# A delta-rule attention kernel: the score product is split into keys with keys, early, and keys with queries and state, late

## The chip, the cores and the metric

The kernel runs on one core of a Trainium2 chip. The metric is the device time of one execution in microseconds (us), from the first to the last instruction. Data are float32, except for the two weight matrices of the second block, which arrive as float64 and are converted inside the kernel.

## The reference, cut to what matters

Two blocks follow each other. The first is a linear attention with a delta rule: 4 batches, 8 heads, 768 time steps, head dimension 48. The second is a two-layer network with a quick GELU on the 3072 x 384 result.

```python
k_n = k / (norm(k) + 1e-6)
for t in range(S):                                   # S = 768
    y[t]  = q[t] @ state                             # state: D x D per batch and head, D = 48
    v_old = k_n[t] @ state
    state = state + beta[t] * outer(k_n[t], v[t] - v_old)
x = y, heads side by side                            # (4*768) x 384
h = x @ w_in                                         # 384 x 2048
out = (h * sigmoid(1.702 * h)) @ w_out               # 2048 x 384
```

The kernel works on chunks of 128 time steps. A **unit** is one chunk of one batch with its 8 heads; there are 6 chunks x 4 batches = 24 units, and units 0 to 3 are the first chunk, where the state is still zero. Inside a chunk the recurrence becomes a triangular system. It needs the products of keys with keys (matrix N, from which 32 x 32 diagonal blocks are inverted), of keys with queries (masked to the part above the diagonal), of keys with the old state (subtracted from the values), and of queries with the old state.

## The kernel before

The start normalizes the keys of units 0 to 3, prepares these four units, and inverts their diagonal blocks (a substitution, one VectorE operation after another). Then a loop of slots runs. Slot n holds the later part of unit n-1, the middle of unit n and the start of unit n+1, the preparation of unit n+4, and pieces of the two-layer network ("filler") in between; each slot has six groups.

```python
W0, W1, WB = 3, 1, (1, 3, 5, 7, 8)       # weight parts to convert: at the start, after the inversion, per slot
NW, NA0, NY, NB0 = 80, 3, 48, 6          # matmuls that only keep TensorE busy; NB0 per group of the first slots

for i in range(B):                        # first loads: keys on SyncE's queue, queries on ScalarE's
    for t, src, dma in ((KN, k, nc.sync.dma_start), (QP, q, nc.scalar.dma_start)):
        nc.vector.memset(t[i][:, :, D:DP], 0.0)
        load(i, ((t, src),), dma)

def prepare(n):
    c, b = units[n]
    kn, qp = KN[n % len(KN)], QP[n % len(QP)]
    kqT = wk.tile([128, NP, 2, 128], F32, tag="kqT", bufs=6)
    for i, src in enumerate((kn, qp)):                       # keys, then queries
        psT = ...                                            # one PSUM bank
        for j in range(NP):                                  # NP = 4 pairs of heads
            pe.transpose(psT[:, j, :], flat[:, j * 128 : (j + 1) * 128], ident)
        act.activation(kqT[:, :, i, :], psT, ACT.Copy)
        yield 0.6
    G = wk.tile([128, H, 2, 128], F32, tag="G", bufs=6)
    for g in range(0, NP, 2):
        ps = [two banks, "psG"]
        for i in range(2):
            for hh in range(2):                              # even and odd heads: partitions 0.. and 64..
                pr = slice(hh * 64, hh * 64 + D)
                pe.matmul(ps[hh][:, i], lhsT=kqT[pr, g + i, 0, :], rhs=kqT[pr, g + i, :, :])   # 256 columns
        act.activation(G[:, 2 * g : 2 * g + 4 : 2], ps[0], ACT.Copy)
        if n < HB or B <= n < 2 * B + HB:
            act.activation(G[:, 2 * g + 1 : 2 * g + 4 : 2], ps[1], ACT.Copy)
        else:
            vec.tensor_copy(G[:, 2 * g + 1 : 2 * g + 4 : 2], ps[1])
        yield 1.0
    nc.sync.dma_start(out=Nd..., in_=G[:, :, 0, :])          # N to DRAM
    nc.sync.dma_start(out=NT[...], in_=Nd...)                # its diagonal blocks back, one per partition
    nc.gpsimd.affine_select(out=G[:, :, 1, :], ...)          # mask of the queries' scores

# class Step (one unit)
def keys(self):                                              # not for the first chunk
    for h in range(H):
        pe.matmul(psK[h % 2][:, j, :], lhsT=self.kqT[self.rows(h), j, 0, :],
                  rhs=ST[self.rows(h), self.b, j * D : (j + 1) * D])                           # 48 columns
    for hh in range(2):
        vec.tensor_tensor(Vh, Vh, psK[hh], op=ALU.subtract)

def slot(n, share):
    for group in range(GR):                                  # GR = 6
        if group == 0:   next(P, None); next(P, None)        # P = prepare(n + 4): transposes
        elif group == 1: together([(B_, 1)], [(A, 2)]); next(P, None)
        elif group == 2: D_ = steps[n + 1] = Step(n + 1, ...); D_.keys(); run(P)
        elif group == 3: together([(A, 3), (D_, 0)], [(B_, 1)])
        elif group == 4: A.queries(); A.outputs()
        else:            together([(B_, 2)], [(D_, 0)]); A.state()
        ...
        more = left // (GR - group)                          # left starts as WB[n + 1]
        run(weights(more)); left -= more                     # convert weight parts
        ... filler ...
        if not queue and n <= HB:
            warm(NB0)
    ...
    load(m, ((KN, k), (QP, q)), ...)                         # m = n + 6

# the start
for b in range(0, B, HB):
    normalize_first(b)
ahead(1, sync)                                               # first three weight parts, one transfer
run(weights(1, None))                                        # convert part 0
first = [prepare(b) for b in range(B)]
for b in range(B + 1):
    if b < B:
        next(first[b]); next(first[b]); warm(NA0)
    if b > 0:
        run(first[b - 1])
run(weights(W0 - 1, None))                                   # convert parts 1 and 2
for b in range(B):
    load_values(b, sync)
...
ahead(2, sync)                                               # fetch further weight parts
run(invert(0))
normalize_first(B, len(KN) - B)
run(weights(W1))
for n in range(-1, len(units) + 1):
    slot(n, ...)
```

A `together` call solves blocks (psU), copies the result (US), multiplies it with the rows below (psR) and subtracts that from the values V on VectorE. Up to slot 1 the instructions of VectorE, ScalarE and TensorE are held in program order. The conversion of a weight part is a handful of VectorE operations (in most parts one on ScalarE); the raw part waits in a staging place inside the buffer of w_out, and a place is free again once the part after it has been converted.

Of the kernel before, what the change touches and what calls it, by code (L numbers as in the profile page):

```python
# [18 lines left out]
def kernel(  # L19
# [37 lines left out]

    W0, W1, WB = 3, 1, (1, 3, 5, 7, 8)
    NA = W0

    NW, NA0, NY, NB0 = 80, 3, 48, 6
    XR = DP - D
# [57 lines left out]
    for i in range(B):  # L120
        for t, src, dma in ((KN, k, nc.sync.dma_start), (QP, q, nc.scalar.dma_start)):
            nc.vector.memset(t[i][:, :, D:DP], 0.0)
            load(i, ((t, src),), dma)

# [87 lines left out]
    def stage(part):  # L212
# [11 lines left out]
        return at, at + 2 * DM  # L224

    def free(part):
        s = stage(part)
        return s is None or all(s[1] <= a or b <= s[0] for a, b in taken.values())

    def fetch(part, dma):  # L230

        if part < parts_in:
            j, f0 = part % KC, part // KC * N_IN
            parts = list(range(part, part + (KC if part < 3 * KC else 1)))
            shape, src = (len(parts), N_IN), moe_w_in[:, f0 : f0 + N_IN]
            dst = w_in[:, j : j + len(parts), f0 : f0 + N_IN]
        else:
            parts = [part]
            shape, src = (1, DM), moe_w_out
            dst = target(part)  # L240
# [75 lines left out]
    def normalize_first(b0, nb=HB):  # L316
# [5 lines left out]
        z = wk.tile([128, 4, nb, H], F32, tag="ksq", name="z", bufs=1)  # L322
        sq = wk.tile([128, nb, H, D], F32, tag="G", name="sq", bufs=6)
        x, y, t, s = (z[:, i] for i in range(4))
        for b in range(nb):
            K = KN[(b0 + b) % len(KN)][:, :, 0:D]
            tt(sq[:, b], K, K, op=mult)
            red(s[:, b], sq[:, b], axis=AX.X, op=add)
        ts(x, s, 1e-30, None, op0=ALU.max)
# [8 lines left out]
        for b in range(nb):  # L338
            K = KN[(b0 + b) % len(KN)][:, :, 0:D]
            tt(K, K, s[:, b].broadcast_to([128, H, D]), op=mult)  # L340

    def prepare(n):
        c, b = units[n]
        kn, qp = KN[n % len(KN)], QP[n % len(QP)]

        kqT = wk.tile([128, NP, 2, 128], F32, tag="kqT", name="kqT", bufs=6)
        for i, src in enumerate((kn, qp)):
            if c == 0:
                psT = ps_seq.tile([128, NP, 128], F32, tag="seq", name="psT")
            else:  # L350
                psT = ps_big.tile([128, NP, 128], F32, tag="big", name="psT")
            flat = src.rearrange("p h d -> p (h d)")
            for j in range(NP):
                pe.transpose(psT[:, j, :], flat[:, j * 128 : (j + 1) * 128], ident)  # L354
            act.activation(kqT[:, :, i, :], psT, ACT.Copy)
            yield 0.6


        G = wk.tile([128, H, 2, 128], F32, tag="G", name="G", bufs=6)
        for g in range(0, NP, 2):  # L360
            if c == 0 and g > 0:
                ps = [ps_moe.tile([128, 2, 2, 128], F32, tag="moe", name="psG") for _ in range(2)]
            else:
                ps = [ps_big.tile([128, 2, 2, 128], F32, tag="big", name="psG") for _ in range(2)]
            for i in range(2):
                for hh in range(2):
                    pr = slice(hh * 64, hh * 64 + D)
                    pe.matmul(  # L368
                        ps[hh][:, i], lhsT=kqT[pr, g + i, 0, :], rhs=kqT[pr, g + i, :, :],
                        start=True, stop=True,  # L370
                    )
            act.activation(G[:, 2 * g : 2 * g + 4 : 2], ps[0], ACT.Copy)  # L372
            if n < HB or B <= n < 2 * B + HB:
                act.activation(G[:, 2 * g + 1 : 2 * g + 4 : 2], ps[1], ACT.Copy)
            else:
                vec.tensor_copy(G[:, 2 * g + 1 : 2 * g + 4 : 2], ps[1])  # L376
            yield 1.0

        Nd = dram.tile([H * NS], F32, tag="Nd", name="Nd", bufs=4)
        nc.sync.dma_start(  # L380
            out=Nd.rearrange("(h r) -> h r", r=NS)[:, 0 : C * C].rearrange(
                "h (p k) -> p h k", k=C
            ),
            in_=G[:, :, 0, :],
        )
        nc.sync.dma_start(
            out=NT[b * NB * H : (b + 1) * NB * H],
            in_=Nd.rearrange("(d r) -> d r", r=NS // NB)[:, 0 : BS * C].rearrange(
                "d (i k) -> d i k", k=C
            )[:, :, 0:BS],  # L390
        )
        nc.gpsimd.affine_select(  # L392
            out=G[:, :, 1, :], in_=G[:, :, 1, :], compare_op=ALU.is_gt, fill=0.0, base=0,
            pattern=[[0, H], [1, 128]], channel_multiplier=-1,
        )
        ready[n] = kn, kqT, G

# [90 lines left out]
    class Step:  # L488
# [6 lines left out]
        def __init__(self, n, xT):  # L495
            self.c, self.b = units[n]
            self.xT = xT
            self.kn, self.kqT, self.G = ready.pop(n)
            self.V, self.XB = loaded.pop(n), inverse.pop(n)
            self.US = US[n % len(US)]  # L500
            self.U = self.US[:, 0 : H * D].rearrange("p (h d) -> p h d", h=H)

        def rows(self, h):
            return slice(h % 2 * 64, h % 2 * 64 + D)

        def keys(self):
            if self.c == 0:
                return
            psK = [bank("psK", (128, NP, D)) for _ in range(2)]
            for h in range(H):  # L510
                j = h // 2
                pe.matmul(  # L512
                    psK[h % 2][:, j, :], lhsT=self.kqT[self.rows(h), j, 0, :],
                    rhs=ST[self.rows(h), self.b, j * D : (j + 1) * D], start=True, stop=True,
                )
            for hh in range(2):
                Vh = self.V[:, hh::2, :]
                vec.tensor_tensor(Vh, Vh, psK[hh], op=ALU.subtract)

        def below(self, blk, h, psR):  # L520
            r = slice(blk * BS, (blk + 1) * BS)
            for k in range(blk + 1, NB):
                u = slice(k * BS, (k + 1) * BS)
                pe.matmul(  # L524
                    psR[u, h, :], lhsT=self.G[r, h, 0, u], rhs=self.U[r, h, :],
                    start=True, stop=True,
                )
# [5 lines left out]
        def solve(self, blk, h, psU):  # L533
            r = slice(blk * BS, (blk + 1) * BS)
            pe.matmul(  # L535
                psU[r, h, :], lhsT=self.XB[r, h, :], rhs=self.V[r, h, :],
                start=True, stop=True,
# [18 lines left out]
        def queries(self):  # L556
            self.psY = [bank("psY", (128, 2, 128)) for _ in range(2)]
            if self.c > 0:
# [3 lines left out]
                    lambda h: ST[self.rows(h), self.b, h // 2 * D : h // 2 * D + DP],  # L562
                    lambda h: self.kqT[self.rows(h), h // 2, 1, :],
                    True,
# [15 lines left out]
        def outputs(self):  # L580
            self.turned(
                (0, 4, 1, 5, 2, 6, 3, 7),
                lambda h: self.US[:, h * D : h * D + DP], lambda h: self.G[:, h, 1, :],
                self.c == 0,
# [93 lines left out]
    steps, xTs, inverting, gT0 = {}, {}, iter(()), []  # L678

    def together(solves, belows):  # L680

# [14 lines left out]
    def slot(n, share):  # L696
# [12 lines left out]
        for group in range(GR):  # L709
            if group == 0:  # L710
                next(P, None)
                next(P, None)
            elif group == 1:
                together([(B_, 1)], [(A, 2)])
                next(P, None)
            elif group == 2:
                if n + 1 < len(units):
                    h = (n + 1) // HB
                    if h not in xTs:
                        xTs[h] = wk.tile([128, KC, NTH], F32, tag="xT", name="xT", bufs=3)  # L720
                    D_ = steps[n + 1] = Step(n + 1, xTs[h])
                    D_.keys()
                run(P)
            elif group == 3:
                together([(A, 3), (D_, 0)], [(B_, 1)])
            elif group == 4:
                if A:
# [12 lines left out]
            ahead_of(inverting, 5 if n % HB == 1 else 4)  # L740
            more = left // (GR - group)
            run(weights(more))
# [8 lines left out]
        if n % HB == 0:  # L751
            run(inverting)
        if n > 0:
            m = n - 1 + len(KN)
            if m < len(units):
                load(m, ((KN, k), (QP, q)), sync if n < B else nc.sync.dma_start)
            if n - 1 + B < len(units):
# [14 lines left out]
    for b in range(0, B, HB):  # L772
        normalize_first(b)
    ahead(1, sync)
    run(weights(1, None))
    first = [prepare(b) for b in range(B)]
    for b in range(B + 1):
        if b < B:
            next(first[b])
            next(first[b])  # L780
            warm(NA0)
        if b > 0:
            run(first[b - 1])
    run(weights(W0 - 1, None))
    for b in range(B):
        load_values(b, sync)
    nc.gpsimd.memset(ST, 0.0)
    for U in US:
# [3 lines left out]
    for i in range(B, len(KN)):  # L792
        load(i, ((KN, k), (QP, q)), sync)
    ahead(2, sync)
# [38 lines left out]
```

## Time and profile before

| what | value |
|---|---|
| time, median of three | 843.53 us (841.94 to 843.6) |
| profiled execution | 838.2 us, mean granted TensorE clock 0.959 |
| busy: TensorE matmul | 780.8 us (93%) |
| busy: VectorE / ScalarE / GpSimd | 489.2 (58%) / 200.3 (24%) / 109.8 us (13%) |
| first operation of the inversion | 41.24 us after the start |
| its last operation (scaling by beta) starts | 66.47 us |
| first solve of a block (psU) | 77.25 us |
| transposes of unit 6, which open slot 2 | 110.02 us |

Shares over the whole span hide that the program has stages. The page's strip of 40 slices shows TensorE idle or at reduced clock in the first seventh and busy throughout after that, so the table gives the moments at which the early stages end. "PE" is TensorE's matmuls, "PEld" its weight loads, "DVE" VectorE, "ACT" ScalarE, "POOL" GpSimd, "SPq" SyncE's DMA queue. In the trace each float32 matmul of the code stands as two instructions, and each float32 transpose as one.

### The profile page before, as it was taken

How to read it: one execution, taken by the hardware profiler on the slowest of the kernel's cores; microseconds unless marked ns; L12 is line 12 of the kernel's file. 1: busy time of each engine (PE TensorE's matmuls, PEld its weight loads, DVE VectorE, ACT ScalarE, POOL GpSimd, SP SyncE). 2: the span in 40 equal slices, each digit the busy share in tenths (PEclk: the TensorE clock that was granted, in tenths of full speed). 3: DMA queues.
4: the chain of work that ended last, by engine and by line, in shares of the span. 5: the costliest groups of instructions: out<-in, count | busy, mean ns of one | idle time of the engine just before them, and what ended most of it. 6: DMA issues, size and time to landing. Idle time of an engine off the chain costs nothing.

```text
span 838.2 us, 18516 instructions
## 1 busy us (share of the span) xinstructions
PE 780.8 (93%) x8036; PEld 569.2 (68%) x8036; DVE 489.2 (58%) x1049; ACT 200.3 (24%) x383; POOL 109.8 (13%) x120
## 2 busy tenths in 40 slices
PE   8307789999899999999999999999999999999998
PEld 7206578766666876866867867867767768677684
DVE  5698779978977484584584592692781851110000
ACT  3201454242221321221321322312312202111020
POOL 2102231151020211121021112102100000000000
PEclk9657879999899999999999999999999999999999
DMA  9698373553214204214214213223122020000000
GB/s 147 156 159 161 79 188 90 111 146 75 51 36 89 63 20 101 53 44 85 52 36 84 61 41 76 44 51 75 27 67 65 3 52 9 10 16 1 24 1 19
DMA packets 160976, 55.95 MB, mean 67 GB/s; under 512 B 128672, under 2 KB 157568, under 8 KB 160896
## 3 DMA queue, kind: packets, MB, share of 16 engines
q1 hardware_dynamic: 154048, 46.02, 27.5%
q0 software_dynamic: 1856, 7.87, 3.0%
q10 hardware_dynamic: 4992, 0.89, 1.0%
q8 instruction: 63, 1.03, 0.5%
q14 instruction: 17, 0.14, 0.1%
HBM read 33.13 MB, written 20.45 MB: 64 GB/s over the span
## 4 chain that ended last, share of the span: by engine, by line
PE 74%; DVE 12%; DMA 7%; issue 3%; POOL 2%; SPq 1%; ACT 0%; ACTq 0%; DVEq 0%; POOLq 0%
PE po L631 28%; PE ph L616 27%; PE psG L368 4%; PE psU L535 4%; PE psY L551 4%; DMA w_out<-in_moe_w_out_dram 2%; PE psK L512 2%; DVE P L104 2%; PE psR L524 2%; PE psT L354 1%; DMA w_out<-in_moe_w_in_dram 1%; DMA QP<-in_q_dram 1%; DVE YB L104 1%; DVE w_in L104 1%; PE psS L573 1%
## 5 line engine op out<-in xcount | busy, mean ns | idle before, releaser
L616 PE MATMUL ph<-xT,w_in 128*128 128x256 f32 (+1 forms) x1248 | 273.9, 373 | 0.8 <-DVE o L638 0.4
L631 PE MATMUL po<-w_out,gT 128*128 128x384 f32 x768 | 268.3, 495 | 1.8 <-DVE w_out L194 1.8
L616 PEld LDWEIGHTS ph<-xT,w_in 128*128 128x128 f32 x1248 | 221.7, 194 | 39.8 <-issue 9.3
L631 PEld LDWEIGHTS po<-w_out,gT 128*128 128x128 f32 x768 | 139.8, 190 | 94.0 <-issue 6.8
L621 ACT ACTIVATE gT<-ph 128x512 f32<-128x512 f32 (+1 forms) x104 | 58.5, 564 | 186.3 <-PE ph L616 186.3
L531 DVE TENSOR_TENSOR V<-V,psR 32x384 f32<-32x384 f32 x87 | 48.3, 556 | 91.5 <-PE psR L524 89.6
L542 ACT COPY US<-psU 32x384 f32<-32x384 f32 x88 | 41.3, 469 | 166.4 <-PE psR L524 148.1
L535 PEld LDWEIGHTS psU<-V,XB 32*32 32x32 f32 x1408 | 50.5, 106 | 30.2 <-issue 21.1
L368 PE MATMUL psG<-kqT 48*128 48x256 f32 x352 | 56.1, 419 | 7.6 <-DVE G L376 4.9
L535 PE MATMUL psU<-V,XB 32*32 32x48 f32 x1408 | 60.5, 204 | 0.0
L524 PE MATMUL psR<-US,G 32*32 32x48 f32 x2080 | 58.2, 203 | 0.0
L638 DVE COPY o<-po 128x384 f32<-128x384 f32 x24 | 13.3, 555 | 75.4 <-PE po L631 75.1
L154 PE MATMUL ps_warm<-ident 128*128 128x256 bf16 x152 | 23.3, 322 | 35.1 <-DVE ps_warm L104 32.8
L524 PEld LDWEIGHTS psR<-US,G 32*32 32x32 f32 x2080 | 49.1, 105 | 1.0 <-issue 0.7
L432 DVE TENSOR_TENSOR P<-NT,YB 64x2 f32<-64x2 f32 (+4 forms) x135 | 45.8, 339 | 4.1
L392 POOL TENSOR_SCALAR_AFFINE_SELECT G<-G 128x1024 f32<-128x1024 f32 x24 | 27.3, 1137 | 158.6 <-DVE G L376 90.4
L304 POOL TENSOR_TENSOR ksq<-KN 128x384 f32<-128x384 f32 x17 | 14.7, 865 | 248.1 <-DMA KN<-in_k_dram 248.1
L436 DVE TENSOR_REDUCE YB<-P 64x2 f32<-64x2 f32 (+4 forms) x135 | 43.4, 321 | 4.5
L368 PEld LDWEIGHTS psG<-kqT 48*128 48x128 f32 x352 | 34.9, 196 | 15.5 <-DVE G L376 5.3
L154 PEld LDWEIGHTS <-ident 128*128 128x128 bf16 x152 | 17.3, 116 | 40.1 <-DVE ps_warm L104 33.5
L372 ACT ACTIVATE G<-psG 128x512 f32<-128x512 f32 x44 | 26.3, 597 | 57.2 <-PE psG L368 57.1
L307 DVE TENSOR_REDUCE ssq<-ksq 128x8 f32<-128x384 f32 x17 | 9.4, 550 | 47.1 <-POOL ksq L304 47.1
(115 smaller groups left out, 743.4 us busy)
## 6 DMA issues: line engine op xcount, KB each, us to landing
Nd<-G SPq DMA_DIRECT2D x24, 512.0 KB, 3.2
w_out<-in_moe_w_out_dram POOLq DMA_DIRECT2D x14, 384.0 KB, 4.0
KN<-in_k_dram SPq DMA_DIRECT2D x24, 192.0 KB, 3.8
V<-in_v_dram SPq DMA_DIRECT2D x24, 192.0 KB, 3.2
out_dram<-o SPq DMA_DIRECT2D x24, 192.0 KB, 1.9
QP<-in_q_dram SPq DMA_DIRECT2D x20, 192.0 KB, 4.0
w_out<-in_moe_w_in_dram SPq DMA_DIRECT2D x6, 576.0 KB, 12.5
NT<-Nd SPq DMA_DIRECT2D x24, 128.0 KB, 2.4
```

The lines of the kernel that those rows point to most:

```text
L104: return lambda *a, **kw: tc.keep_in_program_order(op(*a, **kw))
L154: pe.matmul(ps, lhsT=ones[:, 0:128], rhs=ones, start=True, stop=True)
L368: pe.matmul(ps[hh][:, i], lhsT=kqT[pr, g + i, 0, :], rhs=kqT[pr, g + i, :, :], start=True, stop=True,)
L432: tt(P, diag(Nf, i * BS, [[0, i], [1, i]]), diag(Yf, 0, [[BS, i], [1, i]]), op=ALU.mult,)
L436: red(diag(Yf, i, [[BS, i]]), P, axis=AX.X, op=ALU.add, negate=True)
L524: pe.matmul(psR[u, h, :], lhsT=self.G[r, h, 0, u], rhs=self.U[r, h, :], start=True, stop=True,)
L531: vec.tensor_tensor(self.V[u], self.V[u], psR[u], op=ALU.subtract)
L535: pe.matmul(psU[r, h, :], lhsT=self.XB[r, h, :], rhs=self.V[r, h, :], start=True, stop=True,)
L542: act.copy(self.U[r], psU[r])
L616: pe.matmul(ph[:, u], lhsT=w_in[:, j, f * 128 : (f + 1) * 128], rhs=xT[:, j, t], start=(j == 0), stop=(j == KC - 1),)
L621: act.activation(gT[f0 // FQ][:, f0 % FQ : f0 % FQ + 2, t], ph, ACT.Gelu_apprx_sigmoid)
L631: pe.matmul(po, lhsT=gT[f // FQ][:, f % FQ, i * C : (i + 1) * C], rhs=w_out[:, f, :], start=(f == 0), stop=(f == FC - 1),)
```

## The change

One product of keys with [keys | queries] (256 columns) and one of keys with state (48 columns) become two other products: keys with keys (128 columns), in the preparation, four slots early as before; and keys with [queries | state] (176 columns), one slot early. Queries are therefore transposed only when their own unit comes near, and are loaded later. For units 0 to 2 the queries' scores are made while VectorE does the substitution of the first inversion, in which TensorE has nothing else to do. The purpose is to take the queries out of the path to the first inversion.

With it go smaller edits: the first inversion's evictions are all on ScalarE (`n < 2 * B + HB`), one weight part fewer is converted before the inversion and one more in slot -1 (`W0`, `WB`), parts are spread over a slot with the surplus first (`-(-left // ...)` in place of `left // ...`), half as many TensorE-only matmuls stand in the first slots (`NB0`), and a transfer of three parts waits until all three of its places are free.

```diff
-    W0, W1, WB = 3, 1, (1, 3, 5, 7, 8)
+    W0, W1, WB = 2, 1, (2, 3, 5, 7, 8)
-    NW, NA0, NY, NB0 = 80, 3, 48, 6
+    NW, NA0, NY, NB0 = 80, 3, 48, 3
     for i in range(B):
-        for t, src, dma in ((KN, k, nc.sync.dma_start), (QP, q, nc.scalar.dma_start)):
-            nc.vector.memset(t[i][:, :, D:DP], 0.0)
-            load(i, ((t, src),), dma)
+        nc.vector.memset(KN[i][:, :, D:DP], 0.0)
+        load(i, ((KN, k),))
     def free(part):
-        s = stage(part)
-        return s is None or all(s[1] <= a or b <= s[0] for a, b in taken.values())
+        places = [s for p in together_with(part) if (s := stage(p)) is not None]
+        return all(s[1] <= a or b <= s[0] for s in places for a, b in taken.values())
     def prepare(n):
-        (transposes of keys and queries, psG with 256 columns, four evictions of 128x512)
+        kT = wk.tile([128, NP, 128], F32, tag="kT", name="kT", bufs=6)
+        transposed(kn, kT, c == 0)
+        yield 0.6
+        G = wk.tile([128, H, 128], F32, tag="G", name="G", bufs=6)
+        pool_, tag = (ps_moe, "moe") if c == 0 and b % 2 else (ps_big, "big")
+        ps = [pool_.tile([128, NP, 128], F32, tag=tag, name="psG") for _ in range(2)]
+        for h in range(H):
+            r = slice(h % 2 * 64, h % 2 * 64 + D)
+            pe.matmul(ps[h % 2][:, h // 2], lhsT=kT[r, h // 2, :], rhs=kT[r, h // 2, :], ...)
+        act.activation(G[:, 0::2], ps[0], ACT.Copy)
+        if n < 2 * B + HB:
+            act.activation(G[:, 1::2], ps[1], ACT.Copy)
+        else:
+            vec.tensor_copy(G[:, 1::2], ps[1])
 ...
-        def keys(self):
-            (psK with 48 columns, two subtractions of 128x192)
+        def scores(self):
+            c, S = self.c, slice(128, 128 + D)
+            self.QS = wk.tile([128, NP, 128 + D], F32, tag="QS", name="QS", bufs=3)
+            self.M = wk.tile([128, H, 128], F32, tag="M", name="M", bufs=3)
+            transposed(self.qp, self.QS[:, :, 0:128])
+            if c > 0:
+                St = ST[:, self.b, 0 : NP * D].rearrange("p (j d) -> p j d", j=NP)
+                act.activation(self.QS[:, :, S], St, ACT.Copy)
+            yield
+            n = 128 + D if c > 0 else 128
+            for g in range(0, NP, 2):
+                pool_, tag = (ps_seq, "seq") if g else (ps_big, "big")
+                ps = [pool_.tile([128, 2, 128 + D], F32, tag=tag, name="psQ") for _ in range(2)]
+                for i in range(2):
+                    for hh in range(2):
+                        r = self.rows(hh)
+                        pe.matmul(ps[hh][:, i, 0:n], lhsT=self.kT[r, g + i, :],
+                                  rhs=self.QS[r, g + i, 0:n], ...)
+                for hh in range(2):
+                    hs = slice(2 * g + hh, 2 * g + 4, 2)
+                    if c > 0:
+                        Vh = self.V[:, hs, :]
+                        vec.tensor_tensor(Vh, Vh, ps[hh][:, :, S], op=ALU.subtract)
+                    act.activation(self.M[:, hs, :], ps[hh][:, :, 0:128], ACT.Copy)
+                if g == 0:
+                    yield
+            nc.gpsimd.affine_select(out=self.M, in_=self.M, ...)
 ...
             if group == 0:
                 next(P, None)
-                next(P, None)
+                D_ = steps.get(n + 1) or new_step(n + 1)
+                next(D_.scored, None)
             elif group == 1:
                 together([(B_, 1)], [(A, 2)])
-                next(P, None)
+                next(D_.scored, None)
             elif group == 2:
-                (new Step) D_.keys()
-                run(P)
+                run(D_.scored)
             elif group == 3:
                 together([(A, 3), (D_, 0)], [(B_, 1)])
+                run(P)
-            more = left // (GR - group)
+            more = -(-left // (GR - group))
 ...
-                load(m, ((KN, k), (QP, q)), sync if n < B else nc.sync.dma_start)
+                load(m, ((KN, k),), sync if n < B else nc.sync.dma_start)
+        (and at the end of slot n the queries of unit n + 4)
 ...
     for b in range(B + 1):
         if b < B:
             next(first[b])
-            next(first[b])
             warm(NA0)
         if b > 0:
             run(first[b - 1])
-    run(weights(W0 - 1, None))
+    for b in range(3):
+        load(b, ((QP, q),), sync)
     for b in range(B):
         load_values(b, sync)
+    for b in range(3):
+        run(new_step(b).scored)
+    run(weights(W0 - 1, None))
+    load(3, ((QP, q),), sync)
```

## The prediction

> **What bounds the kernel now.** I read the table by stage first, since shares of the whole span mix stages. Its columns are the stretch in us, its length, busy time (and count) of PE, PEld, DVE, ACT and POOL, the granted clock, the DMA share and GB/s:
>
> ```profile
> 0.00:41.20 41.20, 26.61 (x188) 20.73 (x188) 26.36 (x73) 12.14 (x22) 8.60 (x21) 0.84 0.92 150
> 41.20:67.70 26.50, 1.14 (x6) 0.84 (x7) 24.98 (x51) 0.64 (x1) 0.00 (x0) 0.50 1.20 159
> 67.70:77.20 9.50, 9.06 (x62) 7.02 (x60) 8.91 (x28) 1.45 (x2) 0.00 (x0) 0.75 0.82 150
> 77.20:110.00 32.80, 28.02 (x522) 21.51 (x523) 24.83 (x46) 15.66 (x30) 12.34 (x19) 0.90 0.52 136
> ...
> 250.00:760.00 510.00, 509.57 (x5536) 369.24 (x5535) 281.62 (x585) 113.69 (x216) 58.88 (x51) 1.00 0.23 50
> ```
>
> There are three regimes. Up to 41 us transfers and order bound it; in the substitution VectorE alone works; slots -1 to 1 (77 to 110 us) are a chain of solves in which PE's count contains matmuls that only keep it busy. From 250 us on TensorE has no gap (509.57 of 510). So a microsecond taken from the first 110 us moves the whole rest forward by one, while in the rest only TensorE's own work counts.
>
> Next I looked at why the inversion starts only at 41.24. The timeline of the start, columns start, length, engine, line, operation, count, idle time before:
>
> ```profile
> 24.36 0.43 DVE L104 TENSOR_SCALAR w_in<-w_out 128x512 int32<-128x512 int32 x1 [5.99 <-DMA w_out<-in_moe_w_in_dram]
> ...
> 29.27 1.28 DVE L376 COPY G<-psG 128x512 f32<-128x512 f32 x2
> 29.55 0.30 SPq L386 DMA_DIRECT2D NT<-Nd  x1
> 30.01 3.06 PEld L368 LDWEIGHTS psG<-kqT 48*128 48x128 f32 x14 [5.27 <-DVE G L376]
> 30.01 3.78 PE L368 MATMUL psG<-kqT 48*128 48x256 f32 x14 [4.87 <-DVE G L376]
> 30.62 4.34 SPq L380 DMA_DIRECT2D Nd<-G  x2
> ...
> 35.05 3.19 SPq L386 DMA_DIRECT2D NT<-Nd  x2
> ...
> 41.24 1.22 DVE L104 TENSOR_TENSOR NT<-NT,bI 128x1024 f32<-128x1024 f32 x1
> ```
>
> VectorE stands 5.99 us for the first weights, converts for 4.9 us (24.36 to 29.27), and only then copies two score banks. TensorE waits 4.87 us for those. N of the last units goes out at about 34.6, comes back at about 40.6 (38.24 plus 2.4, the median of NT's transfers), and meanwhile VectorE converts two further parts until 41.24. Both ends meet at the same moment.
>
> **What the Trainium skill says.** The page TensorE: Matmul & The Clock Gate, section Architectural detail, has ScalarE and VectorE as strict first-in-first-out engines. The trace agrees: the copies at 29.27 stood behind the conversion that waited for data. The same page, section LDWEIGHTS, gives a weight load as columns / 1.2 ns, so 107 ns for 128 columns, whatever the rows; its Part 3, The mechanism, says that loads overlap matmuls in flight only in other row groups. The psK group (below) is issued every 57 ns, which fits two row groups, those of even and odd heads, loading side by side. Its section What's actually happening has an idle array at half clock; the trace shows 0.50 in the substitution. The page Perfetto Trace Analysis, section Identifying the Most-Contended Engine, warns that matmul busy share isn't distance from the limit; so below I use distances between starts.
>
> **Part 1, the start (removed: 0.79 MB of queries, their transposes, half of psG).** Four loads of keys and four of queries are 192 KB each (the issue list), three weight parts are 1.57 MB (128 x 512 x 8 bytes each), beta 0.1 MB: 3.25 MB in the first 24.2 us is 134 GB/s, close to the table's 150, so this stretch runs at the transfer rate. Without queries 2.46 MB take 24.2 x 2.46/3.25 = 18.3 us: the weights come 6 us earlier. Keys come earlier by 1 to 2 us (VectorE waits until 6.99 for the second), so all four units are normalized at about 16.5 in place of 18.4. Evictions no longer stand behind conversions. ScalarE then does, from about 14.2, 4 key copies and 8 score copies of 0.6 us, 7.2 us in all, with small waits: the last N leaves at about 22, not 34.6. In the ideal case that starts the inversion 12.5 us earlier, at 28.5. I take off 2.5 us, because SyncE's queue alternates (N out, wait about 3.5 us until it landed, blocks in, next N): with the order of before, the last pair would be issued at about 28. **Inversion at 31, 10 us earlier.** VectorE's two conversions (18.3 to 26.5) are done by then.
>
> **Part 2, the substitution.** Its VectorE work (25 us) is the same. Scores of units 0 to 2: per unit one 0.6 us copy and four copies of 128x256, which I estimate at 0.38 each from the 128x256 copies of xT (371 ns), so 2.1 us of ScalarE, 6.4 in all, after the queries arrive at about 32. This ends before ScalarE is needed for the one copy in the middle of the substitution (12 us after its start). It costs nothing on the path.
>
> **Part 3, slots -1 to 1.** In before 9 conversions of about 2.75 us (89.78 to 92.52, for one) stand in VectorE's order between the subtractions of the solve chain. After, 10 do, +2.75 us; but with the surplus first, a conversion no longer stands before the last subtractions of slots 0 and 1, and slot 0's start is not filled with TensorE work while VectorE waits (it idles 6.86 us before 89.19). Parts 6 to 8 can be fetched only after part 2 is converted, so their 1.57 MB, some 10 us, may land just when wanted: 0 to 3 us of wait. I put the sum at +2 us gained, with an error of 4.
>
> **Part 4, steady slots (TensorE).** Columns are equal: 256 + 48 = 128 + 176. Eight calls are sixteen instructions each. Measured distances: psK 0.92 us for 16 (338.00 to 338.92), 57 ns each; psG 1.03 us for 8 (338.92 to 339.95), 129 ns; together 3.0 us per unit.
>
> ```profile
> L368 PE MATMUL psG<-kqT 48*128 48x256 f32 x352 | 56.1, 419 | 7.6 <-DVE G L376 4.9
> L512 PE MATMUL psK<-ST,kqT 48*128 48x48 f32 x320 | 23.0, 276 | 0.0
> ```
>
> A straight line through 48 and 256 columns gives 85 and 102 ns for 128 and 176: 3.0 us, no gain. A floor of 57 ns set by weight loads with streaming above it gives 1.0 + 1.3 = 2.3. I take 2.8: 0.2 per unit, 4 us over 20 units. Against it, scores of units 3 to 5 move from slack to the saturated part: 3 x (0.44 for four transposes + 1.3, less the keys' 0.92 in two of them) = about 3.5 us. **Net about 0.**
>
> **Other engines per steady unit.** ScalarE loses one 0.6 us copy and gains four of 0.38 and a state copy of about 0.35: +1.25 us, or 25 us over 20 units, which lifts its share from 24% to about 27%. VectorE loses one 0.69 us copy, and two subtractions of 0.35 become four of about 0.23: -0.5 us. Neither sets the end there.
>
> **Sum.** 843.5 - 10 - 2 - 0 = **831.5 us**.
>
> **Rivals.**
> 1. *A weight transfer takes the place of the queries.* The first saturated stretch needs w_out in time; VectorE was busy 19.75 of 20 us between 140 and 160, and PE idle 5 us of 110 between 140 and 250. If staging sets the pace there, the slots of the start come forward but the network waits: half the gain is lost, about 838. For it: parts 6 to 8 are fetched later. Against: each later part is fetched relative to conversions that also move forward.
> 2. *TensorE's floor is the weight load.* Then the new products cost 2.3 us per unit, 0.7 less x 20 = 14 us, and the time is about 821. For it: psK's 57 ns at 48 columns. Against: psG's 129 ns at 256 columns is above its stream, so loads are only partly hidden.
> 3. *The shorter lead stalls steady slots.* Scores are made one slot before use; an eviction on ScalarE and the subtraction now lie between groups 1 and 3. 0.5 us of TensorE idle in 20 slots would eat 10 us: about 841. Against: each group has some 3.5 us of filler (20.8 / 6) and those copies take under 2.
> 4. *The first stage is set by SyncE's alternation alone*: inversion at 34 to 35, gain 6 to 7: 835.
>
> **Range and chances.** The start carries the gain, 5 to 16 us with its reordering; TensorE's term adds -8 to +6. Taken together, 823 to 840 should hold 8 in 10. Faster by 2% means below 826.7: that needs rival 2 at least in part, or the ideal start with all of part 3; 0.22. Slower by 2% would need rival 3 in force without any gain at the start: 0.03. The rest, 0.75, within 2%.
>
> **What would show it.** Right: first weight conversion at about 18; inversion at 28 to 33; no VectorE copy of scores before it; first psU at 65 to 69; unit 6's transposes near 98; psG and psQ together 2.6 to 3.0 us per unit; TensorE still without gaps from 250 us before the end's tail. Wrong: the inversion after 36 (then a wait of SyncE or ScalarE that I misjudged), TensorE idle in steady slots in front of psQ or psU, or a gap in front of the first po products of w_out.

## The result, and the profile after

The changed kernel takes 841.73 us (median of four, 839.73 to 842.71), the kernel before 843.38. The ratio is 0.998, with a 95% interval of 0.996 to 1.000: within 2%, and hardly to be told from no change. The prediction was 831.5, in a range of 823 to 840.

The start did what was predicted. The timeline of the start of the changed kernel (start, length, engine, line, operation, count, idle before):

```profile
18.87 0.43 DVE L104 TENSOR_SCALAR w_in<-w_out 128x512 int32<-128x512 int32 x1 [1.90 <-DMA w_out<-in_moe_w_in_dram]
...
23.71 1.17 SPq L377 DMA_DIRECT2D Nd<-G  x2
...
27.27 2.19 SPq L383 DMA_DIRECT2D NT<-Nd  x2
...
31.71 1.22 DVE L104 TENSOR_TENSOR NT<-NT,bI 128x1024 f32<-128x1024 f32 x1 [5.14 <-DMA NT<-Nd]
```

The first conversion begins at 18.87 (24.36 before), no copy of scores stands behind it, and the inversion begins at 31.71 in place of 41.24. VectorE now waits 5.14 us for the blocks; it was busy until the last moment before.

The table by stage of the changed kernel (stretch, length, busy time of PE, PEld, DVE, ACT, POOL, granted clock, DMA share, GB/s) shows where the gain goes:

```profile
0.00:31.70 31.70, 18.46 (x172) 15.37 (x172) 19.53 (x60) 8.62 (x15) 4.75 (x21) 0.92 0.90 165
31.70:59.30 27.60, 10.52 (x66) 8.40 (x67) 26.07 (x50) 6.27 (x16) 4.09 (x3) 0.50 0.96 132
...
69.70:107.00 37.30, 28.66 (x463) 22.05 (x463) 30.24 (x60) 15.65 (x30) 11.13 (x20) 0.59 0.86 184
...
250.00:760.00 510.00, 502.09 (x5433) 364.47 (x5432) 277.87 (x599) 131.66 (x281) 57.04 (x52) 1.00 0.23 51
```

In the last stretch TensorE was busy 509.57 of 510 us before; now it is 502.09. It idles 7.9 us where it had no gap. The moments of three kinds of events tell when the lead was lost (us from the start of each profile; the last column belongs to an experiment below):

| event | before | changed | changed, copy first |
|---|---|---|---|
| first operation of the inversion | 41.24 | 31.71 | 31.78 |
| its last operation | 66.47 | 58.10 | 58.10 |
| state of unit 0 updated | 115.45 | 108.07 | 108.07 |
| third output tile copied (VectorE, po to o) | 257.38 | 247.63 | 247.40 |
| fifth | 321.22 | 311.21 | 311.72 |
| fifteenth | 622.82 | 621.15 | 613.60 |
| last | 834.74 | 834.27 | 827.61 |

At the fifth tile the changed kernel is 10.0 us ahead, ten slots later 1.7, at the end 0.5. Tiles two apart are compared, because the filler stands elsewhere in every second slot (at the sixth tile the lead is 15.2 us); over the odd tiles from the fifth to the fifteenth it falls in steps: 10.0, 6.7, 6.9, 4.7, 3.8, 1.7. The waits of the changed kernel (engine, line, what it waited for: us in total, times, the longest), of TensorE between 250 us and the end, and of ScalarE over the whole span:

```profile
PE ph L631 <- ACT gT L636: 7.6, 5, 1.6
```

```profile
ACT gT L636 <- PE ph L631: 165.6, 89, 10.4
...
ACT M L527 <- DVE V L526: 82.1, 37, 7.4
```

TensorE waits for gT, the network's activation on ScalarE, which empties a ph bank; in the kernel before it had no such wait there. And ScalarE has a new one: its copy of the scores (M) waits for VectorE's subtraction (V), which reads other columns of the same bank. One slot of the changed kernel, in order of time:

```profile
321.95 0.87 PE L518 MATMUL psQ<-QS,kT 48*128 48x176 f32 x8
...
322.75 4.15 PE L631 MATMUL ph<-xT,w_in 128*128 128x256 f32 x18
...
324.45 0.55 DVE L310 TENSOR_REDUCE ssq<-ksq 128x8 f32<-128x384 f32 x1 [4.49 <-POOL ksq L307]
...
326.76 0.17 DVE L314 TENSOR_SCALAR rn<-rn 128x8 f32<-128x8 f32 x1 [1.75 <-POOL rn L312]
...
327.79 0.75 DVE L526 TENSOR_TENSOR V<-V,psQ 128x96 f32<-128x96 f32 x4
...
328.14 0.66 ACT L527 ACTIVATE M<-psQ 128x256 f32<-128x256 f32 x2 [5.56 <-DVE V L526]
328.68 1.09 ACT L636 ACTIVATE gT<-ph 128x512 f32<-128x512 f32 x2
329.34 2.21 PE L631 MATMUL ph<-xT,w_in 128*128 128x256 f32 x6 [1.64 <-ACT gT L636]
```

Read it from the top: psQ is issued at 321.95 and done before 323. VectorE stands in its own order behind steps of the key normalization that wait for GpSimd, and subtracts at 327.79. ScalarE has waited 5.56 us for that, with two activations in line behind the copy. Both ph banks are full meanwhile, and TensorE stops for 1.64 us. That is the chain I call theory A. The four other gaps of TensorE in front of ph (390.8, 452.6, 514.0 and 576.4 us) lie in slots like this one, two slots apart: each time VectorE waits 3.1 to 3.4 us for GpSimd with the normalization after psQ is done. In the slots between them it is steps of the block inversion that make VectorE 2.8 to 4.1 us late, and there TensorE does not stop in front of ph. Theory A has two rivals: B, ScalarE's 21 us of added work delay the activation, wait or no wait; C, the two new products cost TensorE more than the old ones.

### The profile page after: what moved, and what is told of

Its sections match the earlier page's. It is cut to its first block, busy times and chain, and to the rows that moved or that the text cites. A ratio compares the mean times of both kernels' runs of the same rounds, so it can differ in the third digit from the quotient of the medians.

```text
span 838.0 us, 18659 instructions
## 1 busy us (share of the span) xinstructions
PE 778.5 (93%) x8040; PEld 572.4 (68%) x8040; DVE 485.1 (58%) x1065; ACT 221.4 (26%) x470; POOL 110.3 (13%) x128
## 3 DMA queue, kind: packets, MB, share of 16 engines
q1 hardware_dynamic: 157760, 45.24, 26.4%
## 4 chain that ended last, share of the span: by engine, by line
PE 59%; DVE 22%; DMA 8%; issue 5%; POOL 3%; SPq 2%; ACT 1%; DVEq 0%; POOLq 0%
PE ph L631 23%; PE po L646 20%; PE psU L550 4%; PE psY L566 3%; DVE P L408 3%; DMA KN<-in_k_dram 3%; DVE P L425 2%; PE psG L366 2%; PE psQ L518 2%; DVE YB L429 2%; POOL rn L312 2%; DMA w_out<-in_moe_w_in_dram 2%; DVE P L104 1%; DVE YB L409 1%; DVE NT L409 1%
## 5 line engine op out<-in xcount | busy, mean ns | idle before, releaser
L530 POOL TENSOR_SCALAR_AFFINE_SELECT M<-M 128x1024 f32<-128x1024 f32 x24 | 27.4, 1143 | 266.7 <-ACT M L527 266.7
L527 ACT ACTIVATE M<-psQ 128x256 f32<-128x256 f32 x96 | 32.9, 385 | 88.6 <-DVE V L526 82.1
L425 DVE TENSOR_TENSOR P<-NT,YB 64x2 f32<-64x2 f32 (+4 forms) x135 | 48.9, 362 | 4.1
L518 PE MATMUL psQ<-QS,kT 48*128 48x176 f32 (+1 forms) x384 | 44.0, 349 | 4.9 <-ACT QS L352 4.8
L518 PEld LDWEIGHTS psQ<-QS,kT 48*128 48x128 f32 x384 | 31.9, 206 | 16.8 <-ACT QS L352 6.5
L607 DVE COPY last<-psY 128x128 f32<-128x128 f32 x20 | 5.7, 287 | 55.2 <-PE psY L566 55.0
L408 DVE TENSOR_TENSOR P<-NT,YB 64x1024 f32<-64x1024 f32 (+3 forms) x36 | 31.7, 904 | 0.3
```

Of the source, the lines that this page charges most:

```text
L408: tt(P, a, b, op=ALU.mult)
L425: tt(P, diag(Nf, i * BS, [[0, i], [1, i]]), diag(Yf, 0, [[BS, i], [1, i]]), op=ALU.mult,)
L518: pe.matmul(ps[hh][:, i, 0:n], lhsT=self.kT[r, g + i, :], rhs=self.QS[r, g + i, 0:n], start=True, stop=True,)
L527: act.activation(self.M[:, hs, :], ps[hh][:, :, 0:128], ACT.Copy)
```

## The experiments

### Copy first, subtraction second

```diff
                 for hh in range(2):
                     hs = slice(2 * g + hh, 2 * g + 4, 2)
+                    act.activation(self.M[:, hs, :], ps[hh][:, :, 0:128], ACT.Copy)
                     if c > 0:
                         Vh = self.V[:, hs, :]
                         vec.tensor_tensor(Vh, Vh, ps[hh][:, :, S], op=ALU.subtract)
-                    act.activation(self.M[:, hs, :], ps[hh][:, :, 0:128], ACT.Copy)
```

> The changed kernel with one edit: of the two readers of a psQ bank, ScalarE's copy of the scores stands first and VectorE's subtraction of the state product second. Theory A (the copy waits for the subtraction, VectorE is late with it, the copy holds up the network's activation behind it on ScalarE, and TensorE stands idle for want of a free ph bank): ScalarE's wait for the subtraction, 82 us in the changed kernel, is gone; TensorE's wait for gT falls from 7.6 us to under 1.5; time 834, 832 to 836.5. Theory B (ScalarE's added work of 21 us, not the wait, delays the activation): the work is the same, so 840 to 842.5. Theory C (what the start gained went into more TensorE work in the steady slots): 840 to 842.5 too, with TensorE's idle time gone but its busy time up.

Measured: 832.64 us against 841.71 of the kernel before, ratio 0.9885 (0.9854 to 0.9915), where the changed kernel had 0.998: some 8 us less, with the same work on every engine. The same slot, with the edit:

```profile
323.27 0.87 PE L518 MATMUL psQ<-QS,kT 48*128 48x176 f32 x8
...
324.22 0.66 ACT L524 ACTIVATE M<-psQ 128x256 f32<-128x256 f32 x2 [0.33 <-PE psQ L518]
...
325.72 0.60 ACT L636 ACTIVATE gT<-ph 128x512 f32<-128x512 f32 x1 [0.84 <-PE ph L631]
...
328.06 0.42 DVE L527 TENSOR_TENSOR V<-V,psQ 128x96 f32<-128x96 f32 x2
328.15 0.87 PE L518 MATMUL psQ<-QS,kT 48*128 48x176 f32 x8
...
329.46 0.53 DVE L527 TENSOR_TENSOR V<-V,psQ 128x96 f32<-128x96 f32 x2 [0.98 <-ACT M L524]
```

VectorE is as late as before (328.06), but ScalarE has copied at 324.22 and the activation follows at 325.72. ScalarE's only wait with M over the whole span is now for the product itself:

```profile
ACT M L524 <- PE psQ L518: 25.2, 39, 4.1
```

TensorE's wait for gT is gone from its list, and between 300 and 600 us it is busy 297.57 us where the changed kernel has 292.09 and the kernel before 299.57. The ten slots of the table above take 301.9 us, as in the kernel before (301.6), where the changed kernel took 309.9. Theory A stands; B falls, since ScalarE's work is the same; C falls with the time.

### New keys normalized two groups later

```diff
-            next(K, None)
+            if group >= 2 or n < HB:
+                next(K, None)
```

> The changed kernel with one edit: from slot 2 on the normalization of new keys begins in group 2 of a slot, not in group 0, so that its VectorE steps, which wait for the keys' transfer and for GpSimd, no longer stand in front of the subtractions in VectorE's order. Theory A with the normalization as what makes VectorE late: ScalarE's wait for the subtraction falls from 82 us to under 45, TensorE's idle time of 8 us between 300 and 600 us to under 4; time 835 to 838.5. Theory B (ScalarE's work) and theory C (TensorE's work): 840 to 842.5. If VectorE is late because of the block inversion's steps instead, also 840 to 842.5, with the wait still near 82 us.

Measured: 839.79 us, ratio 0.998 (0.996 to 0.999). ScalarE's wait for the subtraction is 87.4 us, not less, and TensorE's wait for gT again 7.6. But the run doesn't test what it was meant to test. These engines' instructions are held in program order only up to slot 1, and from 261 us on VectorE's operations stand in the same order here as in the changed kernel. The normalization is still ahead of the subtraction, as the slot of the gap at 453.0 us shows:

```profile
449.64 0.55 DVE L310 TENSOR_REDUCE ssq<-ksq 128x8 f32<-128x384 f32 x1 [4.29 <-POOL ksq L307]
451.94 0.17 DVE L314 TENSOR_SCALAR rn<-rn 128x8 f32<-128x8 f32 x1 [1.75 <-POOL rn L312]
...
452.97 0.75 DVE L526 TENSOR_TENSOR V<-V,psQ 128x96 f32<-128x96 f32 x4
```

So that the normalization makes VectorE late in front of TensorE's gaps is read from the traces; that the gaps would go if it stood elsewhere was not tried in any run.

### Both edits

> Both edits together, copy before subtraction and the later normalization. Theory A: the first edit already takes the wait away, so the second adds little: 831 to 836, within 1.5 us of the first alone. If VectorE's lateness also holds up the solves that need the subtracted values (TensorE waiting for V): up to 3 us below the first alone. Theories B and C: 840 to 842.5.

Measured: 828.63 us, ratio 0.9835 (0.981 to 0.986). This version beats both kernels. It is 4 us below the first edit alone, more than I expected, and not for the reason given: unit 1's state is updated at 134.2 us (142.5 with the first edit alone), and from unit 3 on its lead over that kernel stays between 4.9 and 5.8 us. The second edit helps in the first slots, not in the steady ones, and only there could it: VectorE's order differs between these two kernels from 124 to 261 us and not after that.

### The kernel before with only the evictions moved

```diff
-            if n < HB or B <= n < 2 * B + HB:
+            if n < 2 * B + HB:
```

> The kernel before with one edit of the change: the first inversion's score evictions all on ScalarE, as the changed kernel has them; the queries stay where they were. Theory S1 (the earlier start of the inversion, 41.24 to 31.71 us, comes from both, the queries' transfers and the evictions): TensorE's wait of 4.9 us for the copy on VectorE goes, weights still arrive at 24.4, the inversion starts at 35 to 38, time 838 to 841. Theory S2 (it is the queries' transfers alone): inversion at 40 to 42, time 842 to 844. Theory S3 (it is the evictions alone): inversion at 31 to 33, time 833 to 837, as nothing in the steady slots is slower.

Measured: 839.63 us, ratio 0.997 (0.995 to 0.998). The inversion begins at 36.73: theory S1. Of the 9.5 us, 4.5 come from the order of evictions alone and 5 from the rest, that is the queries' transfers, transposes and half products, and one conversion fewer. One line of the kernel before was worth as much as the whole change. And here a lead is kept: it is 3.4 us at the third output tile, 3.3 at the fifteenth and 3.4 at the last, so it is not the steady slots as such that use up what the start gains.

### Reading both parts on one engine

```diff
                     if c > 0:
                         vec.tensor_tensor(Vh, Vh, ps[hh][:, :, S], op=ALU.subtract)
-                    act.activation(self.M[:, hs, :], ps[hh][:, :, 0:128], ACT.Copy)
+                        vec.tensor_copy(self.M[:, hs, :], ps[hh][:, :, 0:128])
+                    else:
+                        act.activation(self.M[:, hs, :], ps[hh][:, :, 0:128], ACT.Copy)
```

with the later normalization.

> The changed kernel with keys later and the copy of the scores on VectorE behind the subtraction, so that a psQ bank (after the first chunk) has readers on one engine only, in the order of the changed kernel. Theory A (the wait of ScalarE for VectorE on a shared bank): no wait of ScalarE for the subtraction, TensorE idle under 3 us between 300 and 600, 828 to 835, although VectorE has some 1.7 us more per unit. If what helped was the order itself (subtraction late, copy early) and not the wait: 838 to 842. If VectorE's extra 34 us make it the next bound: 838 to 846, with TensorE waiting for V in front of psU.

Measured: 843.46 us, ratio 1.001 (1.000 to 1.003). ScalarE's wait and TensorE's wait for gT are both gone, but the time isn't better. The only wait of TensorE between 300 and 600 us is now

```profile
PE psU L552 <- DVE V L526: 3.6, 9, 1.5
```

VectorE, with 33 us more (80 copies of 0.416), holds up the solves directly. The third case is the one that came; theory A's own numbers were missed (3.6 us idle, not under 3, and 843 us, not 828 to 835). TensorE's busy time there is 296.39, against 292.09 in the changed kernel, so the gap did shrink as A says; but between 110 and 250 us this kernel loses 4.7 us more than the one with later keys (idle time and half clock together, counted as below). The vanished waits fit A, and the run shows that one reader is no remedy when that reader is VectorE; as a test of A the first experiment is the clear one.

### Three of the small edits, undone in the best version

```diff
-    NW, NA0, NY, NB0 = 80, 3, 48, 3
+    NW, NA0, NY, NB0 = 80, 3, 48, 6
```

> The best kernel so far (copy first, keys later; 828.6 us) with NB0 back at 6: twice as many TensorE-only matmuls per group in slots -1 to 1. If the small fill costs clock (0.50 between 80 and 100 us in the changed kernel, 0.91 before) and with it time: the clock there rises to 0.8 or more, and the time falls to 825 to 827. If the clock in those slots doesn't matter, because VectorE's order sets them: 828 to 830. If TensorE itself is short of time there: 830 to 833.

```diff
-    W0, W1, WB = 2, 1, (2, 3, 5, 7, 8)
+    W0, W1, WB = 3, 1, (1, 3, 5, 7, 8)
```

> The best kernel so far with W0, WB back at 3 and (1, 3, 5, 7, 8): part 2 converted before the inversion, the fetch of parts 6 to 8 free before it. VectorE stood idle for 5 us before the inversion in the changed kernel, which is as long as a conversion and a half, so the conversion costs nothing there, and the wait of 3.8 us for parts 6 to 8 in slot 0 goes: 824 to 827 if slot 0's wait is on the path. If the conversion pushes the inversion back, or the transfer then competes with the values and queries: 829 to 832.

```diff
-            more = -(-left // (GR - group))
+            more = left // (GR - group)
```

> The best kernel so far with the floor in place of the ceiling: a slot's surplus conversions come last again. By the step of the prediction that gave the reordering about 2 us or more: 830 to 834. If the order within the slot is worth nothing: 828 to 829.5. If early conversions only bring forward a wait for data (3.8 us in slot 0): 825 to 827.5.

Measured: 839.73, 833.57 and 834.89 us (ratios 0.997, 0.990 and 0.992, each give or take 0.003 or less). All three lie above what I expected (the last by 0.9 us). With NB0 = 6 the clock between 80 and 100 us rises from 0.53 to 0.74, and yet unit 0's state comes 2.1 us later. The lead at unit 0 says little about the end. To see where the time goes I cut the stretch from 110 to 250 us into pieces of 5 us and added TensorE's idle time and the time that reduced clock took (length times one minus granted clock):

| kernel (the one before as timed beside the experiments; the changed one was timed beside a kernel before of 843.4) | state of unit 0 | idle, 110 to 250 | half clock, 110 to 250 | time |
|---|---|---|---|---|
| before | 115.4 | 8.3 | 8.6 | 841.7 |
| changed | 108.1 | 5.9 | 9.4 | 841.7 |
| copy first, keys later | 106.8 | 4.8 | 6.4 | 828.6 |
| and NB0 = 6 | 108.9 | 4.8 | 15.6 | 839.7 |
| and part 2 early | 103.9 | 7.5 | 12.6 | 833.6 |
| and surplus last | 104.3 | 10.6 | 9.1 | 834.9 |

From 828.6, the difference in column 2 plus those in columns 3 and 4 gives 839.9, 834.6 and 834.6 for the last three: the measured times within about 1 us. Part 2 early does start the slots 2.9 us sooner, and surplus last 2.4, against my step for it; both lose more than that afterwards. With NB0 = 6 the granted clock is at half for 17 us in which TensorE never stops:

```profile
174.50:182.50 8.00, 7.12 (x88) 4.86 (x82) 5.99 (x14) 3.08 (x8) 5.16 (x5) 0.77 0.29 74
182.50:199.50 17.00, 17.00 (x92) 9.62 (x96) 11.27 (x33) 4.95 (x12) 1.17 (x1) 0.50 0.22 51
199.50:210.00 10.50, 9.27 (x191) 7.75 (x180) 9.26 (x23) 4.09 (x11) 1.09 (x1) 1.00 0.17 52
```

The idle time ahead of it is short, pieces of 1.5 and 0.9 us. So in these three kernels what the edit does in the first 110 us is outweighed by idle time and half clock later. That the edit causes the particular gap was not traced.

### The masks beside the substitution

```diff
     for b in range(3):
-        run(new_step(b).scored)
+        ahead_of(new_step(b).scored, 3)
```

with a `yield` ahead of the mask of units 0 to 2.

> The best kernel so far, with the GpSimd masks of units 0 to 2 moved out of the substitution into the slots of these units. If these three masks hold up VectorE's operations that run beside them (three operations there took 0.4 to 0.8 us longer than their size asks): from the first operation of the inversion to its last one 25.2 to 25.4 us as in the kernel before, not 26.4 to 26.6, and 827 to 828.5 us, at best 1.2 less in all. If the operations were long for another reason: 26.4 to 26.6 still.

Measured: 829.83 us, ratio 0.986 (0.983 to 0.988), and 26.39 us from the first to the last operation. But the trace has the masks where they were, at 37.93, 41.74 and 45.55: the order on GpSimd was chosen without regard to the edit, so this run says nothing on the question. The second try holds the three masks in program order.

> The kernel with copy first and keys later, with the masks of units 1 and 2 really behind other work of GpSimd (their place in its order is fixed now; unit 0's may still run in the substitution, nothing stands before it). If a mask holds up a VectorE operation of two inputs that falls beside it: from the first operation of the inversion to its last one 25.3 to 25.8 us, against 25.2 in the kernel before and 26.4 to 26.6 with all three masks beside it, and only the operation beside unit 0's mask is long. If the operations were long for another reason: 26.4 or more.

Measured: 832.67 us in one run, no faster than the kernel it starts from (828.63), and 25.85 us from the first to the last operation, at the upper end of what was expected. Only unit 0's mask (37.78 to 38.87) still falls into the substitution, and only the VectorE operation of two inputs beside it is long:

```profile
37.75 0.32 DVE L104 TENSOR_REDUCE YB<-P 128x18 f32<-128x162 f32 x1
38.11 0.98 DVE L104 TENSOR_TENSOR P<-NT,YB 128x200 f32<-128x200 f32 x1
...
39.52 0.41 DVE L104 TENSOR_TENSOR P<-NT,YB 128x242 f32<-128x242 f32 x1
```

In the kernel with three masks beside the substitution (copy first, keys later) the 128x200 product is normal and the 128x242 product, which meets the mask there, is long:

```profile
37.29 0.37 DVE L104 TENSOR_TENSOR P<-NT,YB 128x200 f32<-128x200 f32 x1
37.62 1.09 POOL L530 TENSOR_SCALAR_AFFINE_SELECT M<-M 128x1024 f32<-128x1024 f32 x1 [32.24 <-ACT M L524]
37.69 0.36 DVE L104 TENSOR_REDUCE YB<-P 128x20 f32<-128x200 f32 x1
38.09 0.89 DVE L104 TENSOR_TENSOR P<-NT,YB 128x242 f32<-128x242 f32 x1
```

The lengthening follows the mask. The reduction beside it, with one input, is not touched in either.

## Why the prediction was wrong, point by point

**Part 1, right.** Inversion at 31 predicted, 31.71 measured; weights at 18.3, measured 18.87. The split into transfers and evictions holds too, by the fourth experiment.

**Part 2, nearly right.** "It costs nothing on the path": ScalarE was indeed in time, but the masks cost the substitution 1.2 us (26.39 in place of 25.23 us).

**Part 3, too high.** Gained +2 was the step; of the 8.4 us at the inversion's end 7.4 are left when unit 0's state is updated, so it is -1, inside the error given of 4. The first psU is at 67.26 (65 to 69 was the sign), unit 6's transposes at 103.19 (near 98 was). The wait for parts 6 to 8 was 3.8 us, just over the 0 to 3.

**Part 4, the products, roughly right.** The distances in the changed kernel: 16 keys-with-keys instructions in 1.09 us (335.92 to 337.01), 68 ns each; 8 of queries-and-state in 0.80 us (321.95 to 322.75), 100 ns each, 1.6 for 16. Together 2.7 us; I took 2.8. The old pair took 3.0. Rival 2, 2.3 us, is out.

**The step that failed** is Part 4's "Net about 0" with the sentence under the other engines, "Neither sets the end there", and, behind both, the argument by which I set rival 3 aside: "each group has some 3.5 us of filler (20.8 / 6) and those copies take under 2". The copies do take 0.38 us each. But they don't begin when their product is ready. They begin when VectorE has read the same bank, after a wait of up to 7.4 us. TensorE then stands idle in front of ph, five times for 1.3 to 1.6 us, and not in front of psQ or psU, where the prediction would have looked. I added up durations of the new operations and didn't ask in whose order each stands and which of them share a bank. From the fifth to the fifteenth tile TensorE idles 7.9 us, and another 1.7 us go to reduced clock after one of these gaps; the products save about 3 us over these ten slots. Less the 0.4 us that the kernel before idles there, this is 6.2 of the 8.3 us of lead lost. Of the other 2, about 1.5 lie at 319, 444 and 568 us, where some products of ph start 0.29 to 0.45 us apart in place of 0.22; why was not found. Rival 3 named the loss (10 us, to 841) and the range left it just outside.

The Trainium skill had the missing fact. PSUM — Partial Sum Buffer, section PSUM bank collisions raise a hardware error, says that no two engines may access one bank within the same partitions at the same time, and asks to guard it by bank (more finely, by bank and group of 32 partitions), not by address. In the profile ScalarE's copy waits for VectorE although the two read different columns, and with the order turned round VectorE's subtraction waits for ScalarE (the wait of 0.98 us before 329.46 is ended by the copy). The trace agrees: no copy in the changed kernel's slot above starts before its bank's subtraction. In the kernel before, the two evicting engines had a bank each (ps[0] and ps[1]), so nothing of this showed in its profile. No run here puts the two parts into separate banks; that it is the shared bank, and not the shared tile, rests on the page.

With that one order mended, the kernel takes 832.6 us, which is 1.1 us from the number predicted. That it lies so close is partly luck: beside it the kernel before took 841.7, so 9.1 of the 12 us predicted are gained.

## What to carry to other kernels

When a change puts two results into one PSUM bank, ask which engines read them and who reads first: the second reader inherits the first one's place in its queue, and everything behind the second reader inherits it too. Let the engine whose queue feeds the bottleneck read first. And when adding up a change to the start of a kernel, look one stage further: a lead of 10 us shrank to 1.7 in ten slots with, on average, 0.8 us of idle time each.

## What the hardware showed that I had not expected

A GpSimd mask that starts first holds up a VectorE operation of two SBUF inputs beside it by 0.5 to 0.8 us (0.41 to 0.89 and 0.57 to 1.41 us with three masks, 0.37 to 0.98 with one). The reverse is there too: with copy first and keys later the third mask starts at 45.24, while such an operation runs, and takes 1.83 us in place of 1.09:

```profile
44.89 1.23 DVE L104 TENSOR_TENSOR P<-NT,YB 128x1024 f32<-128x1024 f32 x1
45.24 1.83 POOL L530 TENSOR_SCALAR_AFFINE_SELECT M<-M 128x1024 f32<-128x1024 f32 x1 [2.71 <-ACT M L524]
```

In the Trainium skill, SBUF — State Buffer, section SBUF: two separate sides, describes an exclusive lock on a shared port pair, which a VectorE operation with two SBUF inputs and a GpSimd operation that reads SBUF take from each other, whichever starts first keeping it for its whole length; the traces agree.

Short gaps of TensorE can be followed by a cost greater than their own. After the gap of 1.64 us shown above, the changed kernel's clock is lowered although TensorE is busy again:

```profile
330.50:334.00 3.50, 3.50 (x11) 2.79 (x10) 0.00 (x0) 0.02 (x1) 0.99 (x1) 0.57 0.03 5
334.00:338.00 4.00, 4.00 (x91) 3.30 (x90) 1.25 (x2) 2.11 (x4) 0.00 (x0) 1.00 0.22 44
```

The other four gaps of 1.3 to 1.6 us in front of ph are followed by no half clock at all. In all twelve profiles every stretch of half clock inside the run lasts a whole number of steps of 3.41 us: one after this gap, five in the 17 us above. Why one gap is followed by none, another by one step and another by five stays open.
